# A gated mix kernel: the queries' transposed features go through DRAM instead of across partitions on chip

## The chip, the cores and the metric

The kernel runs on one core of one Trainium2 chip. A core has five engines that run side by side, each through its own list of instructions in order: TensorE (PE in the profile, its weight loads PEld), VectorE (DVE), ScalarE (ACT), GpSimd (POOL) and SyncE (SP), which in this kernel issues nearly all DMA transfers. An engine's instruction waits on semaphores that other engines or landed DMAs raise. An instruction that waits holds up everything behind it on the same engine; for SP, this means that a DMA waiting for its data holds up every later DMA of the list. The metric is device microseconds per execution.

## The reference: what is computed

Input x has 2048 rows of 512. The output is `g * a + (1 - g) * b` with a gate g per row.

- Branch a is linear attention with 32 heads of 16. Queries and keys go through a small matrix per head, and then `phi = concat(softmax(p), softmax(-p))`, 32 features per head. `kv = phi_k^T v` and `z = sum(phi_k)` are summed over all rows, and each row's output is `phi_q kv / (phi_q z)`, times `wo`.
- Branch b is a dense layer, Mish, and a dense layer (512 to 1376 to 512).
- g is the sigmoid of a dot product of the row with `gate_w`.

All of it is in float32; the kernel splits each matmul operand into a high and a low part and makes three matmuls of one.

## The kernel before, in words

The work has two stages. Stage A goes over the rows in eight chunks of 256: projections of keys, values and queries (`proj`), the keys' features, the sums kv and z. The projected queries are stored to a DRAM tile `pqd`. Stage B goes over the rows in four blocks (b = 0 to 3) of 512, each with four tiles of 128 rows (t = 0 to 3). In each block TensorE makes branch b (steps `up0` to `up10` and `dn0` to `dn9`, `df`), and for the attention, in two halves h of two tiles each, `nu` (features times kv, written `num<-eT,kvb` in the profile) and four `wo` products.

What feeds `nu` is a chain for every tile t, with these step names:

- `lq` (L552): load the tile's projected queries from `pqd` (`pq<-pqd`).
- `mx`, `mn`, `d0`, `d1`, `E`, `S` (`feat_ops`, L250): VectorE takes maxima, minima and differences, ScalarE the exponentials, VectorE the sums. The tile's features, 128 rows by 1024, stand in `E`; two tiles share one `E` buffer, of which there are two.
- `T`, `D`, `m`, `de`, `rd`, `sc`, `es`: VectorE divides by the sums and the denominator.
- `tr` (L571): VectorE transposes `E` in place in blocks of 32 by 32 (`STREAM_TRANSPOSE`). After this each block is transposed within itself, but the features still have to go to other partitions.
- `mv` (L586), once for each half: moves the blocks of two tiles by DMA from `E` into `eT`, whose partitions are features.
- `nu` (L593), `oh` and `ol` (L604, L609): the matmuls with `kvb`, and the split of their result by ScalarE (high) and VectorE (low, `ohl<-num,ohl`). `nu` of the first half writes one bank with the tag `kv`, and so does the first `wo` product after it. So that product's first matmul waits until `ol` has read the bank.

Beside this stand `gr`, `ge`, `gg` (the gate: a row to DRAM and back, its exponential on ScalarE, three small VectorE operations, L537 to L539), `LX`, `XH`, `XL` (load and split the next block's x: `xraw`, `xbh`, `xbl`), and `fi` (the sum and the store of the output).

The order of everything is written out by hand. `BLOCK0`, `BLOCK1` and `BLOCK` (L61 to L82) are texts of step names; `run` calls them one by one, and every instruction is pinned to its engine's program order. A `+` means the step of the next block, so a block does part of the next block's chain. Two places of these orders matter here. In `BLOCK1` (and in `BLOCK`, for blocks 2 and 3):

```
S3 T3 rS3 D3 m3 de3 rd3 sc3 es3 tr3 lq0+ lq1+ mv1 ... mx0+ mn0+ d00+ d10+ mx1+ mn1+ d01+ d11+ ... E0+ E1+ ge gg
S0+ T0+ ... tr0+ up6 mi6 ... dn5 nu0 nu1 oh0 ol0 ... dn6 wo0 ag0 wo1 ag1 oh1 ol1 tr1+ mv0+
```

and in `BLOCK0`, `tr0`, later `tr1 mv0 lq0+ lq1+`, later `tr2`, then `tr3 mv1` with `lq2+ lq3+` behind it, `tr0+`, then `LX0 LX1`, `tr1+ mv0+`.

Of the kernel before, what the change touches and what calls it, by code (L numbers as in the profile page):

```python
# [8 lines left out]
F32 = mybir.dt.float32  # L9
# [5 lines left out]
P = 128  # L15
S = 2048
D = 512
# [71 lines left out]
def tile_gated_mix(ctx: ExitStack, tc: tile.TileContext, xT, wv, wkT, wqT, bd, w1a, w1b, b1, w2a, w2b, wo, out):  # L89
# [6 lines left out]
    pin = tc.keep_in_program_order  # L96
    V, G_, A_, Sy = nc.vector, nc.gpsimd, nc.scalar, nc.sync

    def mm(*a, **k):
        return pin(nc.tensor.matmul(*a, **k))  # L100

    def T(shape, dt, tag, bufs, name):
        nm[0] += 1
        return sp.tile(shape, dt, name=f"{name}_{nm[0]}", tag=tag, bufs=bufs)

    def k8(name, tag, dt=F32R):
        return T([P, 2048], dt, tag, 2 if tag in ("eT", "E") else 1, name)

    def k4(name, tag, dt=F32):
        return T([P, 1024], dt, tag, {"tx": 2, "oh": 2, "z": 1}[tag], name)  # L110

    def k2(name, tag, dt=F32):
        return T([P, 512], dt, tag, {"pq": 3, "io": 4, "hl": 8}[tag], name)

    def psum(name, tag, bufs={"a": 3, "dn": 4, "kv": 1}):
        nm[0] += 1
        return pp.tile([P, 512], F32, name=f"{name}_{nm[0]}", tag=tag, bufs=bufs[tag])

    def act(out_, in_, fn=AF.Copy, **k):
        return pin(A_.activation(out_, in_, fn, **k))  # L120
# [4 lines left out]
    def hv(ap):  # L125
        return ap.rearrange("p (h f) -> p h f", f=DH)

    def f32(ap):
        return ap.bitcast(F32)
# [69 lines left out]
    def at(key, name, fn):  # L199
        steps.setdefault((key, name), []).append(fn)  # L200
# [10 lines left out]
    xs, Es, vs, psA, Ep = {}, {}, {}, {}, {}  # L211
# [38 lines left out]
    def feat_ops(key, t, src, d):  # L250

        n = str(t)

        def red(name, op):
            d[name] = T([P, H], F32, name, 2, name)
            pin(V.tensor_reduce(d[name], hv(src()), axis=AX.X, op=op))  # L256

        def dd(a):
            if "E" not in d:
                pair = key, t // 2  # L260
                if key == ("A", NCH - 1):
                    d["E"] = k4("E", "oh")
                else:
                    if pair not in Ep:
                        Ep[pair] = k8("E", "E", F32)[:, :].rearrange("p (t x) -> p t x", t=2)
                    d["E"] = Ep[pair][:, t % 2, :]
            E = hv(d["E"][:, a * 512 : (a + 1) * 512])
            if a == 0:
                pin(V.tensor_sub(E, hv(src()), d["mx"][:, :, None].to_broadcast([P, H, DH])))
            else:  # L270
                pin(V.tensor_sub(E, d["mn"][:, :, None].to_broadcast([P, H, DH]), hv(src())))  # L271

        def ss():
            d["S"] = T([P, 2 * H], F32, "Sm", 2, "Sm")
            pin(V.tensor_reduce(d["S"], hv(d["E"][:, :]), axis=AX.X, op=ALU.add))  # L275

        at(key, "mx" + n, lambda: red("mx", ALU.max))
        at(key, "mn" + n, lambda: red("mn", ALU.min))
        at(key, "d0" + n, lambda: dd(0))
        at(key, "d1" + n, lambda: dd(1))  # L280
        at(key, "E" + n, lambda: act(d["E"], d["E"], AF.Exp))
        at(key, "S" + n, ss)
        at(key, "rS" + n, lambda: pin(V.reciprocal(d["S"], d["S"])))

    def scale_by(d, eng):
        pin(eng.tensor_mul(hv(d["E"][:, :]), hv(d["E"][:, :]), d["S"][:, :, None].to_broadcast([P, 2 * H, DH])))  # L286
# [189 lines left out]

    def b_ops(b):
        key = ("B", b)
        U, dn, eTs, num, ohl, io = {}, {}, {}, {}, {}, {}

        def up(i):
            f = ORDER[i]
# [63 lines left out]
        for t in range(4):  # L546
            d = {}

            def lq(t=t, d=d):
                i = 4 * b + t  # L550
                d["p"] = k2("pq", "pq")
                pin(Sy.dma_start(d["p"], pqd[i * P : (i + 1) * P, :]))  # L552

            def tm(d=d):
                d["T"] = k4("T", "tx")
                pin(V.tensor_mul(d["T"], d["E"], B["zb"]))  # L556

            def dsum(d=d):
                d["D"] = T([P, 2 * H], F32, "Dn", 2, "Dn")
                pin(V.tensor_reduce(d["D"], hv(d["T"][:, :]), axis=AX.X, op=ALU.add))  # L560

            def de(d=d):
                d["d"] = T([P, H], F32, "den", 2, "den")
                pin(V.scalar_tensor_tensor(d["d"], d["D"][:, :H], 1e-6, d["D"][:, H:], op0=ALU.add, op1=ALU.add))  # L564

            def sc(d=d):
                sv = d["S"][:, :].rearrange("p (a h) -> p a h", a=2)
                pin(V.tensor_mul(sv, sv, d["d"][:, None, :].to_broadcast([P, 2, H])))

            def tr(d=d):  # L570
                pin(V.transpose(d["E"][:, :], d["E"][:, :]))  # L571

            at(key, f"lq{t}", lq)
            feat_ops(key, t, lambda d=d: d["p"][:, :], d)
            at(key, f"T{t}", tm)
            at(key, f"D{t}", dsum)
            at(key, f"m{t}", lambda d=d: pin(V.tensor_mul(d["D"], d["D"], d["S"])))
            at(key, f"de{t}", de)
            at(key, f"rd{t}", lambda d=d: pin(V.reciprocal(d["d"], d["d"])))
            at(key, f"sc{t}", sc)  # L580
            at(key, f"es{t}", lambda d=d: scale_by(d, V))
            at(key, f"tr{t}", tr)


        for h in range(2):
            def mv(h=h):  # L586
                eTs[h] = k8("eT", "eT", F32)[:, :].rearrange("p (t q x) -> p t q x", t=2, q=4)
                for q in range(4):
                    for k in range(4):
                        o = 64 * (k % 2) + 32 * (k // 2)  # L590
                        pin(Sy.dma_start(eTs[h][o : o + 32, :, q, :], Ep[key, h][32 * q : 32 * q + 32, :, k * 256 : (k + 1) * 256]))  # L591

            def nu(h=h):  # L593
                ev = eTs[h][:, :, :, :].rearrange("p t q (b c) -> p b (t q) c", c=32)
                po = [psum("num", tag) for tag in (("a", "a") if b and h else ("kv", "a"))]
                for bh in range(2):
                    for c in range(4):
                        u = 4 * bh + c
                        for r in range(2):
                            mm(po[r][32 * c : 32 * c + 32, bh * SC : (bh + 1) * SC], kvb[64 * r : 64 * r + 64, u, :], ev[64 * r : 64 * r + 64, u, :, :], start=True, stop=True, skip_group_check=True)  # L600
                for r in range(2):
                    num[h, r] = po[r]

            def oh(h=h):  # L604
                for gp in range(2):
                    ohl[h, gp] = k4("ohl", "oh", F32R)
                    act(ohl[h, gp][:, :512], num[h, gp])

            def ol(h=h):  # L609
                for gp in range(2):  # L610
                    pin(V.tensor_sub(ohl[h, gp][:, 512:], num[h, gp], f32(ohl[h, gp][:, :512])))

            at(key, f"mv{h}", mv)
            at(key, f"nu{h}", nu)
            at(key, f"oh{h}", oh)
            at(key, f"ol{h}", ol)
# [59 lines left out]
    for b in range(NB):  # L676
        b_ops(b)
# [47 lines left out]
    for j in range(2):  # L725
        h, l = [w[:, 2 * j : 2 * j + 2, :].rearrange("p k f -> p (k f)") for w in (wvh, wvl)]
# [94 lines left out]
```

## Time and profile before

| What | Value |
|---|---|
| Median of the three runs | 451.55 us (450.78 to 451.81) |
| The profiled execution's own time | 449.86 us |
| Its span, first to last instruction | 448.1 us |
| TensorE busy, share of the span | 442.7 us, 99% |
| VectorE, ScalarE, GpSimd busy | 312.6, 194.0, 162.2 us |
| Granted TensorE clock | 0.999 |
| DMA traffic | 40.20 MB, 27177 packets |
| HBM read, written | 22.82 MB, 8.40 MB |

Times inside the profile are microseconds from the span's start. A line of a timeline shows start, length, engine, source line, operation, `out<-in`, shapes and a count of merged instructions, and in square brackets the idle time of the engine just before with what ended it. SPq is SP's queue: a DMA's line there is the time of its issue, not of the transfer. The time "to landing" is counted from the start of the issue to the arrival of the data. A list of waits shows who waited for what: the sum, how many times, and the longest.

### The profile page before, as it was taken

The numbers are of one execution on the slowest core, as the hardware profiler recorded it, in microseconds if no ns is written. First come the engines' busy times: TensorE is split into PE (matmuls) and PEld (weight loads), VectorE is DVE, ScalarE is ACT, GpSimd is POOL, SyncE is SP. The second block draws the span as 40 slices with busy tenths as digits, with TensorE's granted clock in tenths as the row PEclk, the third lists the DMA queues.
The fourth block names the chain that finished last, engine by engine and source line by source line (L and its number), as shares of the span: only waits on it lengthen the run. The fifth ranks groups of instructions, "written<-read, shape, count | busy, mean of one in ns | idle before, by whom it ended". The sixth has DMA issues, their size and how long they took to land.

```text
span 448.1 us, 7219 instructions
## 1 busy us (share of the span) xinstructions
PE 442.7 (99%) x2878; PEld 363.5 (81%) x2878; DVE 312.6 (70%) x412; ACT 194.0 (43%) x267; POOL 162.2 (36%) x101
## 2 busy tenths in 40 slices
PE   8999999999999999999999999999999999999997
PEld 7888888888888888778788878888878888887885
DVE  3797658559399999999989998369769329701103
ACT  3644433444325457527165352644262653242330
POOL 3448686677862253511132220214220222221121
PEclk9999999999999999999999999999999999999999
DMA  7721522514511122313433141321231302030002
GB/s 270 272 95 47 191 80 84 191 32 155 190 49 47 48 65 66 93 49 90 147 99 136 40 151 53 88 95 47 66 123 48 94 2 94 17 78 1 0 1 94
DMA packets 27177, 40.20 MB, mean 90 GB/s; under 512 B 6916, under 2 KB 15620, under 8 KB 27144
## 3 DMA queue, kind: packets, MB, share of 16 engines
q1 hardware_dynamic: 26824, 39.35, 28.0%
q8 instruction: 22, 0.36, 0.3%
q10 hardware_dynamic: 288, 0.39, 0.3%
q14 instruction: 11, 0.09, 0.1%
q0 software_dynamic: 32, 0.01, 0.0%
HBM read 22.82 MB, written 8.40 MB: 70 GB/s over the span
## 4 chain that ended last, share of the span: by engine, by line
PE 87%; DVE 9%; SPq 2%; issue 1%; DMA 0%; ACT 0%; DVEq 0%
PE proj L100 27%; PE down L100 23%; PE up L100 22%; PE wo L100 10%; PE num L100 2%; SPq L591 2%; PE kvp L100 1%; PE warm L100 1%; DVE xbl L409 1%; DVE Sm L275 1%; PE fuse L100 1%; DVE E L286 1%; DVE T L556 1%; DVE E L271 1%; DVE den L564 1%
## 5 line engine op out<-in xcount | busy, mean ns | idle before, releaser
L503 POOL TENSOR_TENSOR l<-act,h 128x512 fp32r<-128x512 f32 x44 | 62.6, 1425 | 222.1 <-ACT h L120 203.1
L120 ACT ACTIVATE act<-up,b1s 128x512 f32<-128x512 f32 x44 | 30.2, 687 | 87.6 <-PE up L100 86.7
L324 POOL TENSOR_TENSOR zacc<-zacc,E 128x1024 f32<-128x1024 f32 x16 | 39.7, 2482 | 42.7 <-DVE E L286 41.4
L120 ACT ACTIVATE E<-E 128x1024 f32<-128x1024 f32 x32 | 33.5, 1059 | 41.0 <-DVE E L271 40.9
L286 DVE TENSOR_TENSOR E<-E,Sm 128x1024 f32<-128x1024 f32 x32 | 45.6, 1426 | 1.1
L100 PE MATMUL wo<-woh,ohl 128*128 128x512 f32 x128 | 41.2, 389 | 0.0
L275 DVE TENSOR_REDUCE Sm<-E 128x64 f32<-128x1024 f32 x32 | 38.5, 1204 | 1.5 <-ACT E L120 1.5
L100 PE MATMUL down<-w2ah,h 128*128 128x512 f32 x96 | 37.6, 392 | 0.0
L100 PE MATMUL down<-w2al,h 128*128 128x512 f32 x96 | 37.4, 390 | 0.0
L100 PE MATMUL down<-w2ah,l 128*128 128x512 f32 x96 | 37.4, 389 | 0.0
L256 DVE TENSOR_REDUCE mx<-proj 128x32 f32<-128x512 f32 x16 | 11.0, 689 | 30.7 <-PE proj L100 30.7
L100 PE MATMUL down<-w2bh,h 128*128 128x512 f32 x78 | 30.6, 392 | 0.0
L409 DVE TENSOR_TENSOR xbl<-xraw,xbh 128x1024 fp32r<-128x1024 f32 x8 | 12.0, 1528 | 26.5 <-ACT xbh L120 26.5
L100 PE MATMUL down<-w2bl,h 128*128 128x512 f32 x78 | 30.4, 390 | 0.0
L100 PE MATMUL down<-w2bh,l 128*128 128x512 f32 x78 | 30.3, 389 | 0.0
L120 ACT ACTIVATE h<-act 128x512 fp32r<-128x512 f32 x44 | 27.8, 632 | 1.4
L100 PEld LDWEIGHTS wo<-woh,ohl 128*128 128x128 f32 x128 | 24.0, 188 | 5.0
L120 ACT ACTIVATE io<-wo,g_sb 128x512 f32<-128x512 f32 x16 | 10.9, 689 | 35.3 <-PE wo L100 35.3
L120 ACT ACT_TABLE_LOAD x19 | 24.4, 1283 | 3.8 <-PE up L100 3.5
L100 PE MATMUL up<-xbh,w1ah 128*128 128x512 f32 x96 | 25.8, 390 | 0.0
L100 PE MATMUL up<-xbl,w1ah 128*128 128x512 f32 x96 | 25.7, 389 | 0.0
L100 PE MATMUL up<-xbh,w1al 128*128 128x512 f32 x96 | 25.7, 389 | 0.0
(120 smaller groups left out, 971.5 us busy)
## 6 DMA issues: line engine op xcount, KB each, us to landing
eT<-E SPq DMA_DIRECT2D x128, 64.0 KB, 2.0
xraw<-in_xT_dram SPq DMA_DIRECT2D x15, 512.0 KB, 4.6
pqd<-qs SPq DMA_DIRECT2D x16, 256.0 KB, 3.1
pq<-pqd SPq DMA_DIRECT2D x16, 256.0 KB, 2.9
out_dram<-io SPq DMA_DIRECT2D x15, 256.0 KB, 2.1
raw<-in_w1a_dram SPq DMA_DIRECT2D x3, 512.0 KB, 4.4
raw<-in_w2a_dram SPq DMA_DIRECT2D x3, 512.0 KB, 4.2
wT<-in_wkT_dram SPq DMA_DIRECT2D x4, 256.0 KB, 4.5
```

Source lines behind the costliest of these rows:

```text
L100: return pin(nc.tensor.matmul(*a, **k))
L120: return pin(A_.activation(out_, in_, fn, **k))
L256: pin(V.tensor_reduce(d[name], hv(src()), axis=AX.X, op=op))
L271: pin(V.tensor_sub(E, d["mn"][:, :, None].to_broadcast([P, H, DH]), hv(src())))
L275: pin(V.tensor_reduce(d["S"], hv(d["E"][:, :]), axis=AX.X, op=ALU.add))
L286: pin(eng.tensor_mul(hv(d["E"][:, :]), hv(d["E"][:, :]), d["S"][:, :, None].to_broadcast([P, 2 * H, DH])))
L324: at(key, f"z{t}", lambda d=d: pin(G_.tensor_add(zacc, zacc, d["E"])))
L409: pin(V.tensor_sub(xb[b][1][:, :, sl], kt(raw[h], SC), f32(xb[b][0][:, :, sl])))
L503: pin(G_.tensor_sub(U[i]["l"], U[i]["a"], f32(U[i]["h"])))
L556: pin(V.tensor_mul(d["T"], d["E"], B["zb"]))
L564: pin(V.scalar_tensor_tensor(d["d"], d["D"][:, :H], 1e-6, d["D"][:, H:], op0=ALU.add, op1=ALU.add))
L591: pin(Sy.dma_start(eTs[h][o : o + 32, :, q, :], Ep[key, h][32 * q : 32 * q + 32, :, k * 256 : (k + 1) * 256]))
```

## The change

`tr` now also stores the whole transposed tile, 128 partitions by 1024 values, to a DRAM tile of its own (16 such tiles, `ed`). `mv` makes four loads for each of the two tiles, each filling 32 partitions of `eT` with 4 pieces of 256 values a partition. Before, `mv` made sixteen moves from `E` to `eT`, each with 2 pieces of 256 values for 32 partitions. The step texts are the same.

```diff
-            def tr(d=d):
+            def tr(t=t, d=d):
                 pin(V.transpose(d["E"][:, :], d["E"][:, :]))
+                ed[t] = tc.dram_tile([P, 2 * D], F32, name=f"ed{4 * b + t}")
+                pin(Sy.dma_start(ed[t], d["E"]))
...
             def mv(h=h):
                 eTs[h] = k8("eT", "eT", F32)[:, :].rearrange("p (t q x) -> p t q x", t=2, q=4)
-                for q in range(4):
+                for t in range(2):
+                    src = ed[2 * h + t].rearrange("(q p) x -> p q x", q=4)
                     for k in range(4):
                         o = 64 * (k % 2) + 32 * (k // 2)
-                        pin(Sy.dma_start(eTs[h][o : o + 32, :, q, :], Ep[key, h][32 * q : 32 * q + 32, :, k * 256 : (k + 1) * 256]))
+                        pin(Sy.dma_start(eTs[h][o : o + 32, t, :, :], src[:, :, k * 256 : (k + 1) * 256]))
```

The order of TensorE's, VectorE's, ScalarE's and GpSimd's instructions in the built program is the same before and after. SP's list changes: in each half's place stand two stores and eight loads, the stores where `tr` stands in the step texts, the loads where `mv` stands.

More of the change, by code (lines that the diff above doesn't have):

```diff
@@ L478, in b_ops @@
         key = ("B", b)
-        U, dn, eTs, num, ohl, io = {}, {}, {}, {}, {}, {}
+        U, dn, eTs, num, ohl, io, ed = {}, {}, {}, {}, {}, {}, {}
         def up(i):
```

## The prediction

> **What bounds the kernel now.** I read the page's busy shares first, then the chain that ended last, then the list of waits.
>
> ```profile
> PE 442.7 (99%) x2878; PEld 363.5 (81%) x2878; DVE 312.6 (70%) x412; ACT 194.0 (43%) x267; POOL 162.2 (36%) x101
> PE 87%; DVE 9%; SPq 2%; issue 1%; DMA 0%; ACT 0%; DVEq 0%
> ```
>
> TensorE is busy all the time, so the change can only gain what TensorE waits for `eT`, and lose what new waits it puts in front of TensorE. The chain's 2% of SPq are sixteen issues of `mv`, in one place. The list of waits says how much:
>
> ```profile
> PE num L100 <- DMA eT<-E: 0.8, 1, 0.8
> PEld num L100 <- DMA eT<-E: 0.4, 1, 0.4
> ```
>
> Each occurs once. So the next view is TensorE's timeline at the first halves' `nu` in block 0, with the later places that will matter:
>
> ```profile
> 189.22 0.39 PE L100 MATMUL down<-w2ah,l 128*128 128x512 f32 x1
> 190.44 1.60 PE L100 MATMUL num<-eT,kvb 64*32 64x256 f32 x32 [0.83 <-DMA eT<-E]
> ...
> 197.54 0.39 PE L100 MATMUL wo<-woh,ohl 128*128 128x512 f32 x1
> ...
> 213.95 1.09 PE L100 MATMUL num<-eT,kvb 64*32 64x256 f32 x32
> ...
> 217.83 0.39 PE L100 MATMUL wo<-woh,ohl 128*128 128x512 f32 x1
> ...
> 225.99 1.07 PE L100 MATMUL up<-xbh,w1ah 128*128 128x512 f32 x4
> ...
> 264.16 1.96 PE L100 MATMUL num<-eT,kvb 64*32 64x256 f32 x64
> ...
> 268.94 0.39 PE L100 MATMUL wo<-woh,ohl 128*128 128x512 f32 x1
> ```
>
> The 0.83 us, and 1.60 instead of 1.09 us for the 32 matmuls, are what late `eT` costs: 1.3 us. All other `nu` run without a stop.
>
> **The change part by part.** SP's timeline and the costs of its transfers:
>
> ```profile
> 179.31 10.20 SPq L591 DMA_DIRECT2D eT<-E  x16
> 201.93 10.18 SPq L591 DMA_DIRECT2D eT<-E  x16
> 213.35 7.11 SPq L400 DMA_DIRECT2D xraw<-in_xT_dram  x2
> 238.73 0.94 SPq L552 DMA_DIRECT2D pq<-pqd  x2
> 252.44 10.18 SPq L591 DMA_DIRECT2D eT<-E  x16
> ```
>
> ```profile
> eT<-E SPq DMA_DIRECT2D x128, 64.0 KB, 2.0
> out_dram<-io SPq DMA_DIRECT2D x15, 256.0 KB, 2.1
> raw<-in_wo_dram SPq DMA_DIRECT2D x8, 128.0 KB, 3.1
> xraw<-in_xT_dram SPq DMA_DIRECT2D x1, 512.0 KB, 4.6
> xraw<-in_xT_dram SPq DMA_DIRECT2D x1, 512.0 KB, 3.1
> pq<-pqd SPq DMA_DIRECT2D x2, 256.0 KB, 2.7
> ```
>
> The last three come from the transfers listed for three stretches: an x load right behind two `pq` loads (4.6 us), one alone (3.1 us), and two `pq` loads alone at 238.5 us.
>
> *Removed:* 128 issues, 0.64 us each (10.20 / 16), from SP. *Added:* 16 stores, 0.5 us of issue each (0.94 / 2, `pq` loads, 128 partitions as well), and 64 loads, 0.64 us (the old moves, also 32 partitions). That is 82 us of issue down to 49 us on a queue that idles most of the time. It costs nothing by itself. Landing: a store of 512 KB is not in the trace; the bounds are 2.1 us (a 256 KB store) and 4.6 us, and I take the 3.1 us of a 512 KB transfer alone. A load of 128 KB takes 3.1 us as in the `raw<-in_wo` row, bounds 2.0 (the 64 KB move) and 4.6 us.
>
> [...]
>
> *First half of block 0: a gain.* `mv0` starts when `tr1` ends, at 179.3. After: store 179.31, landed 182.4; the four loads of tile 0 go out meanwhile, as its store went long before; the four of tile 1 from 182.4 to 185.0, the last issued at 184.3 and landed at 187.4. TensorE would take `nu0` at 189.45 (189.22 and one step of 0.23). So the whole 1.3 us are open. The second `mv`, by the same steps from 201.93, lands at 210.0, and `nu1` comes at 213.95 less the gain: covered by 2.6 us.
>
> *But the gain meets the next waits.* VectorE, not late in block 0 because of TensorE, keeps its times, and so does the x load:
>
> ```profile
> 195.88 1.22 DVE L611 TENSOR_TENSOR ohl<-num,ohl 128x512 fp32r<-128x512 f32 x2
> ...
> 216.12 1.27 DVE L611 TENSOR_TENSOR ohl<-num,ohl 128x512 fp32r<-128x512 f32 x2
> ...
> 218.91 1.16 DVE L560 TENSOR_REDUCE Dn<-T 128x64 f32<-128x1024 f32 x1
> ```
>
> ```profile
> 224.23 1.06 ACT L120 ACTIVATE xbh<-xraw 128x1024 fp32r<-128x1024 f32 x1 [5.20 <-DMA xraw<-in_xT_dram]
> ```
>
> The first `wo` matmul waits for the first of the two `ohl` splits: done at 196.49 and 216.75, needed at 197.54 and 217.83, room 1.05 and 1.08 us. The split of x ends at 225.29, and `up0` of block 1 starts at 225.99: room 0.70. Its load can't go earlier, since its buffer waits for VectorE's `Dn`, done at 220.07; it then took some 4.1 us. So the gain that reaches block 1 is 0.7 us; were the load as slow as the 4.6 us row, 0.2, and as fast as the 3.1 us row, 1.0, where `ohl` stops it.
>
> *Block 1: a loss.* The moved stores stand in SP's list where `tr2` and `tr3` stand, ahead of `lq0+` and `lq1+`. Before, SP issued these two loads at 238.73, because only `mv1` behind them waited for `tr3`. After, they queue behind a store that waits for `tr3`. Who waits for them is VectorE, at once:
>
> ```profile
> 251.13 1.25 DVE L571 STREAM_TRANSPOSE E<-E 128x1024 f32<-128x1024 f32 x1
> 252.30 0.65 DVE L256 TENSOR_REDUCE mx<-pq 128x32 f32<-128x512 f32 x1
> ...
> 258.34 0.17 DVE L537 TENSOR_SCALAR ge_sb<-ge_sb 128x4 f32<-128x4 f32 x1 [1.22 <-ACT ge_sb L120]
> ...
> 266.92 1.25 DVE L611 TENSOR_TENSOR ohl<-num,ohl 128x512 fp32r<-128x512 f32 x2
> ```
>
> `tr3` ends at 252.38, the store is issued at 252.44, the first load at 252.94. It lands 2.7 us later if nothing is ahead of it: 255.6, so `mx` is late by 3.3 us. Behind 512 KB on the same queue an x load took 4.6 instead of 3.1 us; 1.5 us more gives 4.8. I take 3.7, nearer the first: most of the load's 2.7 us is its start, which runs beside the store, as even the 64 KB move needs 2.0. The second load comes 0.5 us later and VectorE needs it 2.35 us later, so it adds nothing.
>
> [...]
>
> Does anything absorb the 3.7 us? VectorE's only idle time up to `ohl` is 1.22 us at `ge_sb`, and ScalarE there follows VectorE directly:
>
> ```profile
> 254.77 1.06 ACT L120 ACTIVATE E<-E 128x1024 f32<-128x1024 f32 x1 [1.39 <-DVE E L271]
> 257.16 1.06 ACT L120 ACTIVATE E<-E 128x1024 f32<-128x1024 f32 x1 [1.33 <-DVE E L271]
> ```
>
> So it shifts as a whole. The first `ohl` split ends at 267.55, and `wo0` starts at 268.94: room 1.4 us. TensorE stops for 3.7 - 1.4 = 2.3 us (bounds 1.9 and 3.4). ScalarE's Mish steps behind these exponentials come late by the same 3.7 us, and hold up `nu1` and `dn6` by some tenths; that lies within the 2.3, since `wo0` waits for VectorE's absolute time.
>
> *Blocks 2 and 3: nothing.* In block 2 the same delay occurs, but there VectorE has a long idle time that ScalarE sets, because its exponentials stand behind a Mish that TensorE paces:
>
> ```profile
> 328.40 0.17 DVE L537 TENSOR_SCALAR ge_sb<-ge_sb 128x4 f32<-128x4 f32 x1 [6.31 <-ACT ge_sb L120]
> ```
>
> 6.31 us cover 3.7. Block 3 has no next block. `mv1` as a whole, from the end of `tr3` to its last landing, takes 0.5 (store) + 1.0 (two `pq` issues) + 7 issues of 0.64 + 3.1 = 9.1 us in blocks 1 and 2, where it took 10.2 + 2.0 - 0.6 = 11.6. In block 1 that is 261.5, and `nu` starts at 264.16: covered by 2.0 us even after the gain. The stores put ahead of `LX0` delay that load from 213.35 to 215.6; it lands near 220, and the split of x waits until 224.23 for the other one. Nothing after block 1 gives time back: TensorE has no later wait.
>
> *Sum:* -0.7 + 2.3 = +1.6 us. The profiled execution took 449.86 us (448.1 of span and 1.76 around it), so 451.5 by its account. It lies 1.7 us under the median, 451.55; on the median the forecast is 453.2. Bounds: 451.55 - 1.0 + 1.9 = 452.45 and 451.55 - 0.2 + 3.4 = 454.75.
>
> **The rivals.**
>
> *Faster: VectorE gets ahead.* Some of its operations come out long, and GpSimd's subtractions run beside them:
>
> ```profile
> 210.75 1.16 DVE L564 SCALAR_TENSOR_TENSOR den<-Dn 128x32 f32<-128x32 f32 x1
> ...
> 239.38 1.17 DVE L577 TENSOR_TENSOR Dn<-Dn,Sm 128x64 f32<-128x64 f32 x1
> 240.58 0.19 DVE L564 SCALAR_TENSOR_TENSOR den<-Dn 128x32 f32<-128x32 f32 x1
> 241.45 2.20 DVE L286 TENSOR_TENSOR E<-E,Sm 128x1024 f32<-128x1024 f32 x1
> ...
> 248.74 0.23 DVE L577 TENSOR_TENSOR Dn<-Dn,Sm 128x64 f32<-128x64 f32 x1
> 249.87 1.23 DVE L286 TENSOR_TENSOR E<-E,Sm 128x1024 f32<-128x1024 f32 x1
> ```
>
> If the shifted times keep the two engines apart, block 1's `tr3` ends 0.94 + 0.97 = 1.9 us earlier against TensorE, and the room at `wo0` grows from 1.4 to 3.3 us, the lower end of the delay: no loss. In block 0 the 0.97 us of the first row make VectorE's `Dn`, and with it x, that much earlier, and the room of 0.70 is no longer the limit: a gain of 1.0, where `ohl` stops it. 451.55 - 1.0 = 450.55. It decides where VectorE gains more than 1.8 us in block 1. Against it: TensorE paces ScalarE and so both of these engines in block 1, and all shift alike. 14%.
>
> *No change to tell.* The `pq` loads lie at their lower end and part of VectorE's lengthening goes: a loss of 1.0 and a gain of 0.7 give 451.9. 21%.
>
> *Slower by more: the way through DRAM is late at `nu` as well.* Store and load together took 3.1 + 3.1 us above. If they took 12, `nu0` of block 0 would start at 179.3 + 12 + 1.9 = 193.2, a loss of 2.8 instead of a gain, and block 1's `pq`, behind a store of 6 us, would land at 259.1, late by 6.8: a stop of 5.4. Together 451.55 + 2.8 + 5.4 = 459.8. A loss at `nu0` begins where the two take more than 9.2 us. Against it are all rows of 2.0 to 3.1 us; for it, that no row is a load of bytes stored just before. 10%.
>
> That the change doesn't do what it says is no rival: the built order has the stores and loads where I count them.
>
> **How the numbers follow.** The main case has 55%, 452.45 to 454.75. The measurement tells about 0.2%, 0.9 us, from no change: faster is below 450.65, slower above 452.45. Faster: most of its rival, 0.12; same: the rest of it and the second rival, with an edge of the main case, 0.24; slower: 0.64. The range of 8 in 10 takes in the second rival and the edges of the others: 450.9 to 455.5.
>
> **What would show it.** In the changed profile: no TensorE wait at block 0's first `nu`; in block 1 an idle time of VectorE of 3 to 5 us before `mx<-pq`, ended by the DMA `pq<-pqd`; and TensorE idle 2 to 3 us before block 1's first `wo`, ended by VectorE's `ohl`. The prediction is wrong if SP issues `pq` before `tr3` ends, if VectorE's chain between `mx` and `ohl` shortens, or if `nu` waits for `eT` anywhere.

## The result and the profile after

The changed kernel takes 454.18 us (median of 6 runs, 453.14 to 455.21), the kernel before beside it 450.88 (450.50 to 451.81, 6 runs). The ratio is 1.0069, 95% interval [1.0048, 1.0091]: slower by 3.3 us. Forecast were 453.2 us, +1.6 on the median, with bounds of +0.9 and +3.2. The direction and the place of the loss were right; as a difference, 3.3 us lie just above the upper bound. The time itself lies within the main case's 452.45 to 454.75, but only because the kernel before took 450.88 us in these runs and not the 451.55 that the forecast was added to: that is luck.

The profiled execution took 455.21 us, its span is 453.2, 5.1 us longer than before's. These are the lines of the page and of the list of waits that answer to those of before:

```profile
PE 445.5 (98%) x2878; PEld 364.3 (80%) x2878; DVE 314.1 (69%) x412; ACT 194.0 (43%) x267; POOL 160.1 (35%) x101
PE 66%; DVE 26%; DMA 5%; issue 2%; SPq 0%; ACT 0%; DVEq 0%
ed<-E SPq DMA_DIRECT2D x16, 512.0 KB, 2.9
eT<-ed SPq DMA_DIRECT2D x64, 128.0 KB, 3.5
```

```profile
DVE mx L256 <- DMA pq<-pqd: 7.5, 2, 3.8
PEld wo L100 <- DVE ohl L614: 4.2, 3, 2.5
PE wo L100 <- DVE ohl L614: 2.9, 3, 2.1
PEld num L100 <- ACT act L120: 0.5, 1, 0.5
```

TensorE's waits for `eT` are gone. In their place it waits for VectorE's `ohl`, and VectorE waits twice for `pq`, once in block 1 (3.68 us) and once in block 2 (3.83 us). The chain that ended last now runs for a quarter of the span through VectorE. The store (2.9 us) and the load (3.5) land about where they were put (3.1 and 3.1).

Where the time went shows in the timelines of TensorE, SP and VectorE:

```profile
44.42 1.27 PE L100 MATMUL kvp<-E,v 128*32 128x64 f32 x76
...
189.96 1.09 PE L100 MATMUL num<-eT,kvb 64*32 64x256 f32 x32
...
197.00 0.50 PE L100 MATMUL wo<-woh,ohl 128*128 128x512 f32 x1 [0.28 <-DVE ohl L614]
...
218.17 0.50 PE L100 MATMUL wo<-woh,ohl 128*128 128x512 f32 x1 [0.55 <-DVE ohl L614]
...
226.47 1.07 PE L100 MATMUL up<-xbh,w1ah 128*128 128x512 f32 x4
...
264.64 2.58 PE L100 MATMUL num<-eT,kvb 64*32 64x256 f32 x64
...
272.28 0.80 PE L100 MATMUL wo<-woh,ohl 128*128 128x512 f32 x1 [2.09 <-DVE ohl L614]
```

```profile
245.69 7.76 SPq L573 DMA_DIRECT2D ed<-E  x2
253.51 1.19 SPq L552 DMA_DIRECT2D pq<-pqd  x2
254.81 3.75 SPq L594 DMA_DIRECT2D eT<-ed  x8
```

```profile
251.86 1.25 DVE L571 STREAM_TRANSPOSE E<-E 128x1024 f32<-128x1024 f32 x1
256.79 0.69 DVE L256 TENSOR_REDUCE mx<-pq 128x32 f32<-128x512 f32 x1 [3.68 <-DMA pq<-pqd]
...
262.88 0.17 DVE L537 TENSOR_SCALAR ge_sb<-ge_sb 128x4 f32<-128x4 f32 x1 [1.22 <-ACT ge_sb L120]
...
271.58 1.25 DVE L614 TENSOR_TENSOR ohl<-num,ohl 128x512 fp32r<-128x512 f32 x2
```

Executions start with a little scatter, so stages are compared against the first `kvp` matmul. It stands here at 44.42, and in the profile before:

```profile
44.00 1.72 PE L100 MATMUL kvp<-E,v 128*32 128x64 f32 x108
```

So 0.42 us are to be taken off the times after. Block 0's first `num` then starts 0.90 us earlier than before and is 0.51 us shorter: a gain of 1.4. At `up0` of block 1 (226.47 - 0.42 = 226.05 against 225.99) nothing of it is left. At block 1's `wo0` TensorE is 272.28 - 0.42 - 268.94 = 2.9 us late: 0.6 of it at `num` (2.58 us long instead of 1.96), 2.1 the stop at `wo0`. The remaining 1.7 us come right behind that stop. The profile in stretches (busy time of each engine with its number of instructions, then the granted TensorE clock, the DMA share and GB/s) shows it:

```profile
264.00:269.00 5.00, 4.99 (x76) 2.97 (x75) 4.86 (x8) 3.64 (x7) 2.52 (x2) 1.00 0.02 5
272.20:275.70 3.50, 3.42 (x8) 2.75 (x9) 3.50 (x6) 0.00 (x0) 0.00 (x0) 0.51 0.85 300
275.80:279.00 3.20, 3.20 (x16) 2.63 (x15) 3.03 (x6) 0.69 (x1) 0.00 (x0) 1.00 0.36 120
```

For 3.5 us after the stop TensorE's clock was granted at 0.51: 8 matmuls in 3.5 us, where 16 go in 3.2 us afterwards. At full clock that work would have taken about half as long, so the stretch costs 3.5 x 0.49 = 1.7 us, an estimate from these two numbers. Not all executions have this. Of the 12 timed ones of this kernel (these six and six more below), five show a mean clock of 0.996 and spans of 452.6 to 453.3 us, and seven show 1.000 and 451.3 to 452.2; the medians of the two groups are 1.4 us apart in span and 1.5 in time.

### The profile page after: what moved, and what is told of

Its sections match the earlier page's. It is cut to its first block, busy times and chain, and to the rows that moved or that the text cites. A ratio compares the mean times of both kernels' runs of the same rounds, so it can differ in the third digit from the quotient of the medians.

```text
span 453.2 us, 7154 instructions
## 1 busy us (share of the span) xinstructions
PE 445.5 (98%) x2878; PEld 364.3 (80%) x2878; DVE 314.1 (69%) x412; ACT 194.0 (43%) x267; POOL 160.1 (35%) x101
## 4 chain that ended last, share of the span: by engine, by line
PE 66%; DVE 26%; DMA 5%; issue 2%; SPq 0%; ACT 0%; DVEq 0%
PE proj L100 25%; PE down L100 15%; PE up L100 15%; PE wo L100 8%; DVE Sm L275 2%; DVE E L286 2%; DVE T L556 2%; DVE Dn L560 2%; DVE E L571 2%; DVE E L269 2%; DMA wT<-in_wqT_dram 2%; DVE E L271 2%; DVE den L564 1%; DVE xbl L409 1%; DVE mn L256 1%
## 5 line engine op out<-in xcount | busy, mean ns | idle before, releaser
L503 POOL TENSOR_TENSOR l<-act,h 128x512 fp32r<-128x512 f32 x44 | 60.7, 1382 | 228.7 <-ACT h L120 196.7
L100 PE MATMUL wo<-woh,ohl 128*128 128x512 f32 x128 | 42.7, 402 | 2.9 <-DVE ohl L614 2.9
L286 DVE TENSOR_TENSOR E<-E,Sm 128x1024 f32<-128x1024 f32 x32 | 44.6, 1393 | 1.1
```

What stands on the lines that cost most here:

```text
L503: pin(G_.tensor_sub(U[i]["l"], U[i]["a"], f32(U[i]["h"])))
```

## The experiments

Theory A: the loss is the two `pq` loads of block 1, queued on SP behind stores that wait for `tr2` and `tr3`; the way through DRAM itself is hidden. Rival B: the way through DRAM, its transfers and their traffic, costs time by itself. Each kernel was timed beside the kernel before on the same chip.

### The loads ahead of the stores

```diff
-    ... mx3 mn3 d03 d13 up1 mi1 hi1 lo1 E2 E3 ... tr2
-    up2 mi2 hi2 lo2 dn0 S3 ... es3 tr3 lq0+ lq1+ mv1 up3 ...
+    ... mx3 mn3 d03 d13 up1 mi1 hi1 lo1 lq0+ lq1+ E2 E3 ... tr2
+    up2 mi2 hi2 lo2 dn0 S3 ... es3 tr3 mv1 up3 ...
```

> The changed kernel with one edit: in block 1 the two loads of projected queries for the next block stand ahead of the stores, in SP's list. Theory A (the loss is these two loads queued behind a store that waits for the transposes; stores and loads through DRAM themselves are hidden): VectorE no longer waits for pq in block 1, TensorE no longer stops before block 1's first wo, the granted clock is 1.00 throughout, and the time is 450.0 to 451.2, no slower than before at 450.9. Theory B (the round trip through DRAM, or its traffic, costs the time by itself): the time stays at 453 to 455, the stops only move.

Measured: 450.51 us against 450.87, ratio 0.9993 [0.9982, 1.0004], no difference. VectorE goes on without a stop in block 1:

```profile
252.44 1.25 DVE L571 STREAM_TRANSPOSE E<-E 128x1024 f32<-128x1024 f32 x1
253.61 0.65 DVE L256 TENSOR_REDUCE mx<-pq 128x32 f32<-128x512 f32 x1
```

The whole 3.3 us are gone with the two loads moved, and 16 stores and 64 loads through DRAM still run. B falls. In block 2 the two loads still stand behind the stores and VectorE waits 3.7 us; this costs nothing, as the prediction said.

### Two stores, and nothing read from them

The kernel before, with one addition in `tr`:

```diff
+                if b == 1 and t >= 2:
+                    pin(Sy.dma_start(tc.dram_tile([P, 2 * D], F32, name=f"ed{4 * b + t}"), d["E"]))
```

> The kernel before, with its moves on chip, and only the two stores of block 1's third and fourth tile added at their transposes; nothing reads them. Theory A: VectorE waits 3 to 4.5 us for pq in block 1 although no feature goes through DRAM, TensorE stops 2 us and more at block 1's first wo, and the time is 453 to 455.5. Theory B: two stores of sixteen, and no load, cost at most an eighth of the 3.3 us: below 451.5.

Measured: 453.65 against 450.87, ratio 1.0060 [1.0044, 1.0077]. All features move on chip, and the loss is there:

```profile
255.97 0.69 DVE L256 TENSOR_REDUCE mx<-pq 128x32 f32<-128x512 f32 x1 [3.67 <-DMA pq<-pqd]
```

```profile
271.47 0.50 PE L100 MATMUL wo<-woh,ohl 128*128 128x512 f32 x1 [1.68 <-DVE ohl L613]
```

TensorE's stop is 1.68 us and not the 2 us expected, and the clock stays at 0.999 or 1.000 in all six runs. Two stores in two places of SP's list, 1 MB in all, cost 2.8 us. By itself this could still be the traffic of the two stores; but the kernel with the loads in front has the same two stores and loses nothing.

### More work for TensorE ahead of the wait

```diff
-    ... es1+ dn6 wo0 ag0 wo1 ag1 oh1 ol1 tr1+ mv0+ dn7 up8 ...
+    ... es1+ dn6 dn7 wo0 ag0 wo1 ag1 oh1 ol1 tr1+ mv0+ up8 ...
```

> The changed kernel, with the late pq loads kept, but TensorE makes block 1's dn7 (twelve matmuls, 2.7 us) before wo0 and not after wo1. Theory A: VectorE still waits 3 to 4 us for pq, but the wait at wo0 has 2.7 us of cover more: at most 0.5 us of it is left, the granted clock is 1.00 there, and the time is 450.5 to 452. Theory B: moving TensorE's work changes nothing, 453 to 455.

Measured: 452.25 against 450.87, ratio 1.0033 [1.0020, 1.0047], 0.25 us over the range that theory A gave. The wait at block 1's `wo0` is gone although `pq` is as late as ever (VectorE waits 3.82 us for it), and a new one has come:

```profile
278.86 1.21 PE L100 MATMUL up<-xbh,w1bh 128*128 128x512 f32 x4 [0.78 <-ACT io L120]
```

`up8`, now directly behind `wo1`, waits for ScalarE to copy a product out of its bank. Block 1's `num` still takes 2.72 us instead of 1.96. Together that is 1.5 us, about the 1.4 that are left. So the order gives the time back only in part; it does show that `wo0` was where TensorE paid most.

### Block 0 alone

In `tr` and `mv` the new way stands under `if b == 0`, the old moves under `else`.

> The way through DRAM in block 0 alone, moves on chip in blocks 1 to 3. Theory A: block 0's first num no longer waits for eT (a gain of 1.0 to 1.3 us there), the most of which is given back at block 0's wo products, where VectorE is not earlier; the time is 450.2 to 451.2. Theory B: about a quarter of the 3.3 us is lost in each block, 451.5 to 452.

Measured: 450.41 against 450.87, ratio 0.9990 [0.9979, 1.0000]. Block 0 loses nothing. It gains next to nothing either, although its first `num` doesn't wait for `eT`; there is a wait for `ohl` at `wo0` instead, as theory A has it:

```profile
190.08 1.09 PE L100 MATMUL num<-eT,kvb 64*32 64x256 f32 x32
...
197.14 0.50 PE L100 MATMUL wo<-woh,ohl 128*128 128x512 f32 x1 [0.30 <-DVE ohl L621]
```

### Is the slow clock the stop's doing?

Theory C: a stop of some 2 us or more makes the granted clock fall. Theory D: the slow stretch was chance. One kernel shortens the stop and one lengthens it; the changed kernel runs again beside them. The first puts a part of `dn7` under a name of its own ahead of `wo0`:

```diff
+                    at(key, "dp7" if b == 1 and i == 7 and t < 1 else ..., lambda i=i, t=t: down(i, t))
-    ... es1+ dn6 wo0 ag0 ...
+    ... es1+ dn6 dp7 wo0 ag0 ...
```

> The changed kernel with the late pq loads kept, but the first three of dn7's twelve matmuls (0.68 us) go before block 1's wo0. This shortens TensorE's stop there from 2.1 to about 1.4 us. If a stop of about 2 us makes the granted clock fall after it (theory C), the clock stays at 1.00 in every run, the matmuls of wo0 take 0.39 us, and the time is 452.5 to 453.5: the shorter stop is paid for by what dn7 no longer covers later, but the slow stretch of 1.7 us is gone. If the slow stretch in the changed kernel was chance (theory D), half the runs show 0.996 again and times scatter up to 455.

The second moves the loads behind `mv1`:

```diff
-    ... tr3 lq0+ lq1+ mv1 up3 ...
+    ... tr3 mv1 lq0+ lq1+ up3 ...
```

> The changed kernel with block 1's two pq loads moved behind the eight loads of mv1 as well, which makes them about 4 us later. TensorE's stop before block 1's first wo grows by the same 4 us, to some 6 us. Theory C: the granted clock falls in every run, 0.996 or lower, and the stretch at low clock is at least as long as in the changed kernel; time 458 to 460. Theory D: the clock is 1.00 in about half of the runs; time 456 to 460 in two groups. Theory A needs the time to grow by about 4 us over the changed kernel's, 454.2.

The third is the changed kernel:

> The changed kernel once more, beside the others on the same chip. Time 453 to 455; its runs fall in two groups, clock 1.000 at about 453.3 and clock 0.996 at about 455.0.

| Kernel | Stop in its profile | Clock of the timed runs | Median | Ratio to before |
|---|---|---|---|---|
| stop shortened | 1.41 us at `wo0` | 0.999 or 1.000 in 6 of 6 | 452.51 | 1.0045 [1.0031, 1.0060] |
| two stores (above) | 1.68 us at `wo0` | 0.999 or 1.000 in 6 of 6 | 453.65 | 1.0060 [1.0044, 1.0077] |
| changed, again | 2.10 us at `wo0` | 1.000 in 4 of 6, 0.996 in 2 | 454.42 | 1.0084 [1.0065, 1.0104] |
| loads later still | 3.70 us at `num` | 0.992 to 0.995 in 4 of 4 | 457.94 | 1.0162 [1.0144, 1.0181] |

```profile
272.15 0.50 PE L100 MATMUL wo<-woh,ohl 128*128 128x512 f32 x1 [2.10 <-DVE ohl L614]
```

```profile
268.99 1.03 PE L100 MATMUL num<-eT,kvb 64*32 64x256 f32 x2 [3.70 <-ACT act L120]
```

```profile
268.90:272.00 3.10, 2.80 (x32) 0.82 (x32) 3.06 (x4) 2.85 (x6) 2.27 (x2) 0.53 0.00 0
272.00:276.00 4.00, 4.00 (x16) 3.09 (x10) 3.83 (x7) 0.00 (x0) 0.24 (x1) 0.51 0.01 4
```

The first row is the changed kernel's again: a stop of 2.10 us, and its clock stayed at 1.00 behind it, where the first profile had 2.09 us and 0.51. The other rows are of the kernel with the loads later still: a stop of 3.7 us, in another place than I expected (the second half's `num`, which waits for ScalarE's Mish to read its bank), and the clock at 0.53 and 0.51 from the end of the stop until about 276, some 7 us. Its 457.94 us lie just under the 458 to 460 that theory C gave. A stop's length is known from one profile of each kernel only, the clock from every run. By these, the runs follow C: the mean clock stayed at 0.999 or 1.000 in the 12 runs of the kernels with stops of 1.4 and 1.7 us, and fell in 5 of 12 runs with 2.1 us and in 4 of 4 with 3.7 us. Two kernels of the next section (the second and third there) stop in block 0 and bear this out:

```profile
222.00 0.51 PE L100 MATMUL wo<-woh,ohl 128*128 128x512 f32 x1 [2.18 <-DVE ohl L614]
```

```profile
223.43 0.64 PE L100 MATMUL wo<-woh,ohl 128*128 128x512 f32 x1 [2.19 <-DVE ohl L611]
```

The mean clock of the first is 0.996 in 5 of its 12 runs, though not in the profiled one. That of the other, whose features move on chip, is 0.995 or 0.996 in 5 of 6, its profiled one among them (0.996): two `wo` matmuls behind the stop take 1.05 us there (at 224.29), where two in the same profile took 0.62 (at 204.65). Why equal stops of 2.1 to 2.2 us go either way, these runs don't show.

### Where the gain of block 0 went

Two kernels change block 0's order, on top of the loads ahead of the stores. The first:

```diff
-    ... mi8 hi8 lo8 dn6
+    ... mi8 hi8 lo8 dn6 dn7
-    up9 mi9 hi9 lo9 dn7 up10 ...
+    up9 mi9 hi9 lo9 up10 ...
-    ... dn9 wo2 ag2 wo3 ag3 df0 fi0 df1 fi1 df2 ...
+    ... dn9 df0 df1 wo2 ag2 wo3 ag3 fi0 fi1 df2 ...
```

> The kernel with the pq loads ahead of the stores in block 1, and in block 0 TensorE makes dn7 before wo0, and the first two df products before wo2, so that VectorE's ohl is not waited for. If the gain of block 0 was given back at ohl alone, TensorE enters block 1 0.7 to 1.0 us earlier than before and the time is 449.6 to 450.2. If the split of the next x (xbh, which waits for VectorE's Dn) stands right behind it, TensorE stops there instead, and the time is 450.2 to 451.0 as without this edit.

Measured: 451.15 against 450.55, ratio 1.0003 [0.9992, 1.0014], no difference (the median is just over the second of the two ranges). TensorE stopped 0.87 us at `wo2` for `ohl` all the same, and 0.67 us at `up0` for `xbh`. The second also moves `T1+ rS1+ D1+ LX0 LX1` ahead of `ol1` and all four `df` ahead of `wo2`:

> The way through DRAM with the pq loads ahead of the stores in block 1, and block 0's order changed further: VectorE makes T and Dn of the next block's second tile before the second ohl, so that the next x load can go 1.8 us earlier (its buffer waits for Dn), and TensorE makes dn7 before wo0 and all four df products before wo2. If ohl and xbh were the two places that took block 0's gain back, both waits are gone and the 0.7 to 1.0 us reach block 1: time 449.6 to 450.3 against 450.7 of the kernel before. If the way through DRAM has another cost that cancels it, the time is 450.5 or more.

Measured: 451.85 against 450.60, ratio 1.0032 [1.0018, 1.0047], slower, where a gain was expected if the two waits were all. The same order on the kernel before, with its moves on chip:

> The kernel before, its moves on chip, with only block 0's order changed in the same way (T and Dn before the second ohl, dn7 before wo0, df before wo2). It keeps the 1.3 us wait for eT at block 0's first num. If what the previous kernel gains comes from the earlier arrival of eT, this one takes 450.5 to 451.3, as the kernel before; if it comes from the order alone, this one is as fast as the previous one.

Measured: 454.49, ratio 1.0090 [1.0074, 1.0107], 3.2 us over the upper end of what was expected. In both, TensorE stops 2.2 us at `wo2`, and the runs with the clock near 0.996 add to the time (452.75 to 453.46 us against 451.10 to 452.02 in the first, 454.35 to 455.31 against 453.68 in the second). The cause, read from the rows, is in this order: it moved `wo0` and `wo1` behind `dn7`, ScalarE's copies `ag0` and `ag1` with them, and the exponentials `E0+ E1+` stand behind these copies, so VectorE idled (0.83 us in the one profile, 2.56 in the other). Two more kernels therefore put the exponentials first:

```diff
-    ... lq2+ lq3+ wo0 ag0 wo1 ag1 E0+ E1+ S0+ ...
+    ... lq2+ lq3+ E0+ E1+ wo0 ag0 wo1 ag1 S0+ ...
```

> As the kernel with block 0's further order (way through DRAM, pq loads ahead of the stores, dn7 before wo0, T and Dn before the second ohl, df before wo2), but ScalarE makes the two exponentials of the next block before the two copies of wo0 and wo1, so that they don't wait for products that were moved later. VectorE should no longer idle 2.6 us at Sm in block 0, TensorE no longer stop 2.2 us at block 0's wo2, and the 0.7 to 1.3 us of the earlier eT reach block 1: 449.3 to 450.2 against 450.7 before. If another wait takes their place (a bank of the tag a, or xbh), 450.4 to 451.5.

> The kernel before with its moves on chip and only the same order of block 0 as the previous kernel. It keeps the wait of 1.3 us at block 0's first num. If the previous kernel's advantage is the earlier eT, this one is 1.0 to 1.3 us slower than it; if the order alone makes it, the two are the same within 0.4 us.

| Kernel, the same order of block 0 | Median | Before beside it | Ratio |
|---|---|---|---|
| through DRAM, `pq` loads first | 449.62 | 450.65 | 0.9969 [0.9957, 0.9981] |
| moves on chip | 450.55 | 450.65 | 0.9999 [0.9986, 1.0012] |

```profile
44.96 0.75 PE L100 MATMUL kvp<-E,v 128*32 128x64 f32 x38
...
190.49 1.09 PE L100 MATMUL num<-eT,kvb 64*32 64x256 f32 x32
...
225.61 1.07 PE L100 MATMUL up<-xbh,w1ah 128*128 128x512 f32 x4
```

These rows are of the first of the two. Neither of the two has a stop at a `wo` any more. Against its `kvp`, 0.96 us later than before's, `up0` of block 1 starts in the first at 224.65 and not at 225.99: 1.3 us earlier, nearly the whole gain of 1.4. In the second, the list of waits has the old one:

```profile
PE num L100 <- DMA eT<-E: 0.9, 1, 0.9
```

So the way through DRAM is worth 0.9 us here, a little under the 1.0 to 1.3 expected, once the loads it held up go first and block 0 can use the earlier `eT`; the order alone is worth nothing. The two kernels differ in the place of the `pq` loads too, but in the second VectorE never waits for `pq`, so their place has nothing to give it. The first is the one version that is faster than the kernel before clear of noise, by 0.3%.

## Why the prediction was right or wrong

*The cost of the DMAs themselves: right.* Stores landed in 2.9 us, loads in 3.5, no `num` of the changed kernel waited for `eT`, and with the loads in front (first experiment) the whole way was free. The rival of a late way through DRAM falls. The prediction's lower bound for the store, the 2.1 us of `out_dram`, left out a row: the page of the kernel before also has 3.1 us, for the stores of 256 KB to `pqd`:

```profile
pqd<-qs SPq DMA_DIRECT2D x16, 256.0 KB, 3.1
```

*The place of the loss: right.* SP issued `pq` behind the store, at 253.51. The delay of VectorE was put at 3.7 us, a choice between 3.3 and 4.8, and is 3.68. Two stores alone bring it about; two loads moved take it away. Block 2's wait was hidden, as forecast.

*The gain of 0.7 us: failed.* The step that failed says that VectorE keeps its times in block 0. It kept them as far as the first `ohl` and no further. Of the 1.4 us gained at `num`, `wo0` kept 197.54 - (197.00 - 0.42) = 0.96, as `ohl` stopped it there (0.28 us); the prediction's 0.70 at the split of x was never reached, since the rest was lost at the second `ohl`. That came 217.44 - 0.42 - 216.12 = 0.9 us later than before. The rows of VectorE and GpSimd tell why, here of the changed kernel:

```profile
212.78 1.10 DVE L568 TENSOR_TENSOR Sm<-Sm,den 128x64 f32<-128x64 f32 x1
...
217.44 1.27 DVE L614 TENSOR_TENSOR ohl<-num,ohl 128x512 fp32r<-128x512 f32 x2
```

```profile
212.52 1.28 POOL L503 TENSOR_TENSOR l<-act,h 128x512 fp32r<-128x512 f32 x1 [0.21 <-POOL l L503]
```

and of the kernel before:

```profile
212.34 0.22 DVE L568 TENSOR_TENSOR Sm<-Sm,den 128x64 f32<-128x64 f32 x1
212.59 1.22 DVE L286 TENSOR_TENSOR E<-E,Sm 128x1024 f32<-128x1024 f32 x1
```

```profile
212.88 2.08 POOL L503 TENSOR_TENSOR l<-act,h 128x512 fp32r<-128x512 f32 x1 [1.02 <-issue]
```

Before, VectorE's long product started first, and GpSimd's subtraction took 2.08 us. After, TensorE and with it the subtraction came earlier against VectorE (the subtraction by 212.88 - (212.52 - 0.42) = 0.78 us); it took 1.28, and VectorE's small product took 1.10 in place of 0.22. The two now ran side by side, the subtraction until 213.80 and the small product from 212.78 to 213.88; before, the small product had ended at 212.56, ahead of the subtraction. My rival in which VectorE gets ahead rested on such lengths changing, and here it went the other way: TensorE came earlier and VectorE later. The 0.88 us by which the small product is longer are the 0.9 us. That the subtraction beside it made it longer is my reading of the rows; no run shows it alone. Tried is that the gain returns in the order of block 0 that gives TensorE work ahead of `ohl` and VectorE the next block's `T` and `Dn` first.

*The stop of 2.3 us: too small by half a microsecond.* From `up0` to `wo0` block 1 lost 2.9 - 0.1 = 2.8 us. The delay was sized right and the room of 1.4 us was not: VectorE itself was later against TensorE than before. `tr3` ended at 253.11 - 0.42 = 252.69, 0.3 us after 252.38, and between `mx` and `ohl` another 0.2 us were lost. The rows of VectorE in block 1 show some operations longer than before (one `E<-pq,mx` 1.73 us instead of 0.68) and some shorter (one `E<-E,Sm` 1.23 instead of 2.20), which nearly balance; what sets these lengths was not tried.

*A term that was missing: the clock.* The prediction counted a stop as its own length. In 5 of 12 runs the clock fell, which cost 1.7 us in the profile of one of them. The five have a median of 455.19 us, the seven at 1.000 one of 453.67, which is 2.8 and 3.1 us above the kernel before beside them (450.88 and 450.55).

In the prediction's terms the sum is +0.1 for block 0 instead of -0.7, +2.8 for block 1 instead of +2.3, and 1.7 in five of twelve runs, 0.7 in the mean, for the clock: 3.6 us against the 3.3 measured.

## What to carry to other kernels

The stores added to SP's list, which wait for their data, held up what stands behind them (two loads, issued at 253.51 instead of 238.73), and the cost was not their own. When a DMA is added to an engine's list, look for what stands behind it there and was issued early until now, and put that first. Before counting a gain in front of TensorE as saved, ask which engines' waits it runs into next; here three rooms of 0.7 to 1.1 us stood behind it, and at one of them VectorE came 0.9 us later than before. A stop of TensorE cost more than its length here: the clock fell in 5 of 12 runs with a stop of 2.1 us, which cost an estimated 1.7 us more in the profile of one of them, and in 4 of 4 with 3.7 us.

## What was unexpected in the hardware

The granted TensorE clock fell to 0.51 for 3.5 us after a stop of 2.09 us in one profile and stayed at 1.00 after 2.10 us in another of the same kernel. Issues to 32 partitions took 0.64 us each from SBUF in block 0 of the kernel before (10.20 / 16) and about 0.47 us in block 1 from DRAM (3.75 / 8). A load of 128 KB from the tile stored just before landed in 3.5 us (the median), and the 256 KB loads from `pqd` in block 1, right behind a 512 KB store, landed in 3.3 us, against 2.7 in the kernel before, at 238.73 with no store ahead. One of VectorE's small products of 128 by 64 took 0.22 us before the change and 1.10 after it, with GpSimd's subtraction beside it the second time.
